# Attention scores and products with V on small TensorE tiles, with P transposed on VectorE, in a fused attention and MoE kernel

## The chip, the cores and the metric

The kernel runs on one core of a Trainium2 chip. The metric is the device time of one execution in microseconds; before the change the median of three runs is 1303.9 (1302.64 to 1307.83).

## The reference, cut to what matters

Eight batches, eight heads, 576 positions, 64 dimensions per head, all float32. The attention is causal by blocks of 64 positions, so a query block i sees the keys of blocks 0 to i.

```python
B, H, S, D = q.shape                      # 8, 8, 576, 64
scores = (1.0 / np.sqrt(D)) * np.matmul(q, k.transpose(0, 1, 3, 2))
scores = np.where(block_i >= block_j, scores, -1e9)      # blocks of 64
attn = np.exp(scores - scores.max(-1, keepdims=True))
attn = attn / (attn.sum(-1, keepdims=True) + 1e-09)
x = np.matmul(attn, v)                    # -> 4608 tokens x 512
h = np.maximum(x @ w_in, 0.0)             # 512 -> 2048
x = h * h @ w_out                         # 2048 -> 512
# then a soft mixture: 32 slots from all tokens, 8 experts on 4 slots each, slots back to tokens
```

## The kernel before, in words

The work is written as a list of operations, each with an engine, a cost in ns, what it reads and writes, and a due time; `Program.order` (L95) plays them through a model of the engines and gives one static order per engine. Among the operations that are ready, an engine takes the one with the earliest due time. The order of TensorE, VectorE, ScalarE and SP is therefore fixed before the run, and a late operand stalls whatever stands behind it on its engine.

Three kinds of work are interleaved. The MLP runs over 12 chunks of 384 tokens and, in each, over 16 slots of 128 hidden units. A slot is 12 matmuls into the bank HB (`slot_h`, L647: the weight and the activation are each split into a high and a low fp32r part, three products for each of four parts), the relu and square on ScalarE, a new split on VectorE (L656, L658), and nine matmuls of 512 columns into three banks (`slot_o`, L672). Slots are due 5 units apart (`t_at`, L793). The low parts of the weights are read again from memory for each slot (L640, `WL`, three buffers).

The attention runs as jobs of two heads, four jobs per batch (`job`, L362); from batch 2 on there are 24 whole jobs (L829 to L832), due 6 slots apart, some slots ahead of the MLP chunk that needs their tokens. A job loads q and k transposed for both heads (L381) and V (L392, L396); makes a rounded copy and a residue of q and k (L400, L403); makes the scores of query tiles of 64 and 128 rows as two fp32r products each (L437); takes negated row maxima on VectorE (L460), exponentials with row sums on ScalarE (L476), scales P by the reciprocal of the sums on either engine (L492, L493); transposes P in 25 blocks of 128x128 on TensorE (L513), copies them from PSUM (L516, L517); and multiplies with V in float32: two 64x64 products for query block 0 (L529), products with 64 output rows for one head beside the other (L539), and full-array ones for the diagonal blocks (L547). The result goes to `xr` (L554), from which `x_split` (L613) makes the chunk's operands. Four PSUM banks (pool "w") serve all jobs and the mixture, `moe2` (L698), which runs once per chunk with three-tile products (L727, L779).

After the last chunk come the experts and the output, bound by the loads of the expert weights at first (L943); `keep_warm` (L990) puts idle transposes into the gap there.

Of the kernel before, what the change touches and what calls it, by code (L numbers as in the profile page):

```python
# [38 lines left out]
class Op:  # L39
    __slots__ = ("alts", "eng", "cost", "fn", "due", "n", "nwait", "pred", "succ", "start", "end", "grp", "take",  # L40
                 "give", "nbytes", "waits", "cls")


class Program:
# [17 lines left out]

    def add(self, alts, r=(), w=(), due=0.0, grp=None, take=False, give=False, nbytes=0, after=(), waits=(), sets=None, cls=None):

        o = Op()
        o.alts = alts if isinstance(alts, list) else [alts]
        o.due, o.n, o.cls = due, len(self.ops), cls
        o.succ, o.grp, o.take, o.give, o.nbytes, o.waits = [], grp, take, give, nbytes, waits
        pred = dict.fromkeys(after, True)
        if grp is not None:  # L70
            w = tuple(w) + (grp,)
# [12 lines left out]
        for k in r:  # L84
            self.readers.setdefault(k, []).append(o.n)
        for k in w:
            self.last_w[k] = o.n
            self.readers[k] = []
        o.pred = pred
        self.ops.append(o)  # L90
        if sets is not None:
            self.events.setdefault(sets, []).append(o.n)
        return o.n

    def order(self, banks):  # L95
# [6 lines left out]
        ready = {e: [] for e in engs}  # L102
        dma_free = 0.0
        bank_at = {k: [0.0] * n for k, n in banks.items()}
        parked = {k: [] for k in banks}
        ops = self.ops

# [42 lines left out]
        while True:  # L150
            best, be = None, None
            for e in engs:
                if ready[e]:
                    t = free[e]
                elif future[e]:
                    t = max(free[e], future[e][0][0])
                else:
                    continue
                if best is None or t < best:
                    best, be = t, e  # L160
            if be is None:
                break
            t = best
            while future[be] and future[be][0][0] <= t:
                _, n = heapq.heappop(future[be])
                heapq.heappush(ready[be], (ops[n].due, n))
            _, n = heapq.heappop(ready[be])
            o = ops[n]
            if o.take:
                at = bank_at[o.grp.pool]  # L170
                i = min(range(len(at)), key=lambda j: at[j])
                if at[i] == float("inf"):
                    parked[o.grp.pool].append(n)
                    continue
                if at[i] > t:
                    heapq.heappush(future[be], (at[i], n))
                    continue
                o.grp.bank = i
                at[i] = float("inf")
            o.start = t  # L180
            load[be] -= o.cost
            if be == "sp" and o.cost:
                free[be] = t + 475.0
                dma_free = max(dma_free, t + 1160.0) + o.nbytes / 360.0
                o.end = dma_free + 900.0
            else:
                o.end = run_pe(t, o.cost) if be == "pe" else t + o.cost
# [25 lines left out]
def c_mm(n):  # L213
    return max(109.0, n / 2.4 + 13)


def c_mm4(n):

    return 4 * max(53.0, n / 2.4) + 56

# [11 lines left out]


def c_tt(n):
    return 66 + 1.04 * n


def emit(tc, qk, v, vd, w, phi, w1, w2, jsel, gsel, out):
    nc = tc.nc
# [119 lines left out]
    def parts(i):  # L359
        return range(2) if i == 4 else range(1)  # L360

    def job(L, b, p, ti, due0, due1, plain=False):  # L362
# [137 lines left out]
        for gi, g, bats, at in plan(ti):  # L500
# [23 lines left out]
            if g[0] == 0:  # L524
                c = at[(2, 0, 0)]

                def mm(gr=gr, c=c):
                    for h in range(2):
                        pe.matmul(bank(gr)[64 * h:64 * h + 64, 0:64], L.VD[0:64, 1 - h, 0:64],  # L529
                                  L.PT[0:64, c + 64 * h:c + 64 * h + 64], start=True, stop=True)  # L530
                prods.append((c_mm4(64), mm, [c // 64, c // 64 + 1], K("VD")))
            for kt in range(g[-1]):
# [8 lines left out]
                prods.append((c_mm4(w_), mm, [x for c in cs for x in range(c // 64, (c + w_) // 64)], K("V")))  # L541
            for i in g:
                if i:
                    c = at[(2, i, i)]

                    def mm(gr=gr, i=i, c=c, o=Q0[i] - q_, last=i == g[-1]):
                        pe.matmul(bank(gr)[:, o:o + 128], L.VD[:, i + 1], L.PT[:, c:c + 128], start=False, stop=last)  # L547
                    prods.append((220, mm, [c // 64, c // 64 + 1], K("VD")))
            for x, (cost, mm, pts, vk) in enumerate(prods):
                pr.add(("pe", cost, mm), r=[vk] + [K("PT", y) for y in pts], grp=gr, take=(x == 0),  # L550
                       waits=old if x == 0 else ())
            r0 = (b % 2) * S + q_
# [26 lines left out]
    def w_decode(ft, due, to, after=()):  # L579

        lt, lk = to
        for j in range(2):
            t, rk = raws(ft, j)

            def part_(x, t=t):
# [8 lines left out]

            pr.add(("act", c_act(N, True), lambda c=c, part_=part_: act.activation(c, f(part_(1)), AF.Abs)),
                   r=rk, w=[ck], due=due)
            pr.add(("act", c_act(N, True), lambda q_=q_, part_=part_: act.activation(q_, part_(0), AF.Copy, scale=2.0 ** -29)),
                   r=rk, w=[qk_], due=due)
# [99 lines left out]
    def moe2(c, m, due):  # L698
# [25 lines left out]
        for k in range(KT):  # L724
            def mm(k=k, g=g):
                for t in range(NTT):
                    pe.matmul(bank(g)[32 * t:32 * t + 32, 0:128], ph[:, k], xT[:, k, t * 128:(t + 1) * 128],  # L727
                              start=(k == 0), stop=(k == KT - 1))
            pr.add(("pe", 270, mm), r=YAK + ["ph"], grp=g, take=(k == 0), due=due)
        M, nM, sE = T("M"), T("nM"), T("sE")  # L730
# [49 lines left out]
        pr.add(("pe", 912, mm), r=[("X2", t) for t in range(NTT)] + ["ET"], grp=g, take=True, due=due)  # L780
        if m == 0:
# [15 lines left out]
    lane_init(L0)  # L797
    lane_init(L1)
    lane_b = []
    for n in range(2):  # L800
# [74 lines left out]
    one = ident[0:1, 0:1]  # L875
    lR = [("a", nm, h) for h in range(2) for nm in ("hk", "hq", "ql")]
    lF = [("a", "V"), ("a", "VD")] + [("a", "P", h, i, z_) for h in range(2) for i in range(5) for z_ in parts(i)]
# [3 lines left out]
    aR = []  # L881

    def in_R(i):
        if not aR:
            aR.append(cp.tile([128, 6 * S], F32, name="aR2", tag="aR"))
        return aR[0][:, 1024 * i:1024 * (i + 1)]

# [106 lines left out]

    keep_warm(36, HB, "HB", due + 200)
    z = (NCH - 1) % 2
# [233 lines left out]
def layout(inp):  # L1230
# [7 lines left out]
    kq = np.stack([kk.reshape(B * H, S, D), q.reshape(B * H, S, D)], axis=1).transpose(0, 3, 1, 2).reshape(B * H, D, 2 * S)  # L1238
    kq = c(np.concatenate([kq, kq], axis=1))
    vb = v_.reshape(B * H // 2, 2, 9, 64, D)  # L1240
    vf = vb[:, :, 0:8].reshape(-1, 2, 4, 2, 64, D).copy()
# [18 lines left out]
    return dict(qk=kq, v=vf, vd=vdiag, w=w, phi=ph, w1=w1, w2=w2, jsel=J.reshape(96, 64), gsel=G.reshape(128, 2, 96))  # L1260

# [15 lines left out]
```

## Time and profile before

| | us |
|---|---|
| median of 3 runs | 1303.9 |
| the profiled execution | 1306.84 |
| its span, first to last instruction | 1305.1 |
| TensorE busy (share of the span) | 1255.4 (96%) |
| VectorE busy | 764.9 (59%) |
| ScalarE busy | 714.6 (55%) |
| mean granted TensorE clock | 0.984 of 2.4 GHz |

Busy time counts matmuls from start to modelled end, and they overlap, so sums of durations are more than the time they take; the chain of work that ended last gives each line the time that it adds. Shares of busy time are means over stretches with different limits; the stretches are read one by one. Durations of VectorE and ScalarE instructions hold some latency that the next one overlaps.

### The profile page before, as it was taken

Reading aid. Unit: us, or ns where it says so; the run is one execution under the profiler, and the core shown is the slowest. Engines: PE = TensorE matmul, PEld = TensorE weight load, DVE = VectorE, ACT = ScalarE, POOL = GpSimd, SP = SyncE. Lnnn points to the kernel's source line nnn. Section 1 sums busy time; section 2 is a strip of 40 time slices with the busy share of each in tenths; the row PEclk is TensorE's granted clock in tenths of the full one; section 3 lists DMA queues with packets and bytes.
Section 4 is the critical chain, followed back from the end, with each engine's and each line's share of the span. In section 5 each row is a group of like instructions: output and inputs, shape, how many; then the busy total and the mean of one; then the engine's idle time right before and its main releaser. Section 6 shows DMA issues by size and latency. Waiting matters only on the chain.

```text
span 1305.1 us, 21721 instructions
## 1 busy us (share of the span) xinstructions
PE 1255.4 (96%) x7877; PEld 1067.6 (82%) x7877; DVE 764.9 (59%) x2429; ACT 714.6 (55%) x1811; POOL 2.7 (0%) x14
## 2 busy tenths in 40 slices
PE   6879899999999999999999999999999999999994
PEld 5657788888888898888888898888888898989843
DVE  7998899846556555555557555555557543232213
ACT  6786797745555555546555545446555544232324
POOL 0000000000000000000000000000000000000000
PEclk8988999999999999999999999999999999999998
DMA  6588668443443334343433343443443336456899
GB/s 191 196 276 275 207 215 286 155 155 117 143 136 116 118 137 131 130 147 117 144 134 118 111 143 131 131 146 120 141 134 121 109 123 226 161 193 239 291 376 339
DMA packets 97643, 224.42 MB, mean 172 GB/s; under 512 B 30337, under 2 KB 42369, under 8 KB 97537
## 3 DMA queue, kind: packets, MB, share of 16 engines
q1 hardware_dynamic: 97536, 223.05, 50.4%
q8 instruction: 62, 1.02, 0.3%
q14 instruction: 45, 0.36, 0.1%
HBM read 204.40 MB, written 18.61 MB: 171 GB/s over the span
## 4 chain that ended last, share of the span: by engine, by line
PE 79%; DVE 12%; ACT 3%; DMA 3%; issue 1%; SPq 0%; ACTq 0%; DVEq 0%
PE HB L647 26%; PE O L672 26%; PE B L437 6%; PE B L512 5%; PE B L539 5%; PE B L547 3%; DVE anm L460 2%; DMA aF<-in_qk 1%; DVE aR L403 1%; PE B L712 1%; PE B L727 1%; ACT aF L476 1%; PE B L779 1%; DVE MG L658 1%; DVE X L602 1%
## 5 line engine op out<-in xcount | busy, mean ns | idle before, releaser
L647 PE MATMUL HB<-MX,W 128*128 128x384 f32 x1536 | 436.3, 343 | 4.7 <-ACT R L653 4.6
L672 PE MATMUL O<-W,MG 128*128 128x512 f32 x1152 | 338.4, 399 | 1.5 <-DVE MG L656 1.5
L647 PEld LDWEIGHTS HB<-MX,W 128*128 128x128 f32 x1536 | 281.6, 189 | 11.7 <-ACT R L653 5.4
L647 PE MATMUL HB<-MX,WL 128*128 128x384 f32 x768 | 261.6, 341 | 0.4 <-DMA WL<-wlo_d 0.2
L476 ACT ACTIVATE aF<-B,anm 128x288 f32<-128x288 f32 (+4 forms) x338 | 166.1, 496 | 159.8 <-DVE anm L466 152.2
L672 PEld LDWEIGHTS O<-W,MG 128*128 128x128 f32 x1152 | 210.1, 189 | 36.6 <-DVE MG L656 2.1
L656 DVE CAST MG<-R 128x384 fp32r<-128x384 f32 x158 | 56.3, 356 | 276.7 <-ACT R L654 276.5
L653 ACT ACTIVATE R<-HB 128x384 f32<-128x384 f32 x192 | 93.9, 489 | 162.2 <-PE HB L647 162.0
L672 PE MATMUL O<-WL,MG 128*128 128x512 f32 x576 | 167.5, 395 | 0.0
L460 DVE TENSOR_REDUCE anm<-B 128x1 f32<-128x288 f32 (+4 forms) x338 | 150.2, 449 | 7.9 <-PE B L437 1.2
L647 PEld LDWEIGHTS HB<-MX,WL 128*128 128x128 f32 x768 | 144.7, 188 | 5.9 <-issue 2.7
L437 PE MATMUL B<-aR 128*128 128x288 f32 (+5 forms) x704 | 136.6, 308 | 9.0 <-ACT aR L400 8.7
L516 ACT COPY aF<-B 128x512 f32<-128x512 f32 (+2 forms) x201 | 103.5, 537 | 60.9 <-PE B L512 59.5
L437 PEld LDWEIGHTS B<-aR 128*128 128x128 f32 (+1 forms) x704 | 109.8, 189 | 23.5 <-ACT aR L400 9.1
L512 PE MATMUL B<-ident,aF 128*128 128x128 f32 x768 | 117.9, 278 | 11.4 <-ACT aF L476 5.1
L672 PEld LDWEIGHTS O<-WL,MG 128*128 128x128 f32 x576 | 108.0, 188 | 24.8 <-issue 1.0
L512 PEld LDWEIGHTS B<-ident,aF 128*128 128x128 f32 x768 | 93.2, 143 | 26.8 <-ACT aF L476 6.9
L658 DVE TENSOR_TENSOR MG<-R,MG 128x384 fp32r<-128x384 f32 x192 | 106.5, 555 | 10.2 <-DVE MG L656 0.9
L403 DVE TENSOR_TENSOR aR<-aF,aR 64x576 fp32r<-64x576 f32 (+6 forms) x136 | 93.2, 687 | 8.9 <-ACT aR L400 6.4
L654 ACT ACTIVATE R<-R 128x384 f32<-128x384 f32 x163 | 85.8, 526 | 3.6
L539 PE MATMUL B<-aF 128*64 128x256 f32 (+1 forms) x792 | 86.2, 349 | 0.0
L492 DVE TENSOR_SCALAR aF<-aF,ari 128x192 f32<-128x192 f32 (+4 forms) x216 | 75.3, 377 | 1.8
(233 smaller groups left out, 1171.3 us busy)
## 6 DMA issues: line engine op xcount, KB each, us to landing
WL<-wlo_d SPq DMA_DIRECT2D x187, 512.0 KB, 3.3
aF<-in_qk SPq DMA_DIRECT2D x24, 1152.0 KB, 5.2
aF<-in_v SPq DMA_DIRECT2D x32, 256.0 KB, 2.8
Wr<-in_w SPq DMA_DIRECT2D x16, 512.0 KB, 4.8
aF<-in_w SPq DMA_DIRECT2D x13, 512.0 KB, 5.9
YA<-in_w SPq DMA_DIRECT2D x11, 512.0 KB, 4.6
call<-in_w SPq DMA_DIRECT2D x11, 512.0 KB, 4.5
wlo_d<-W SPq DMA_DIRECT2D x11, 512.0 KB, 5.3
```

What stands on the lines that cost most here:

```text
L403: return ("dve", c_tt(n), lambda: dve.tensor_sub(dst, a, b_))
L437: pr.add(("pe", cost, lambda a=a, k_=k_, n=n, bc=bc, j=j, rows=rows: pe.matmul(bank(gr)[rows, bc:bc + n], a, k_, start=(j == 0), stop=bool ...
L460: pr.add(("dve", c_tt(n), lambda gr=gr, n=n, bc=bc, x=x: dve.reduce_max(L.nm[:, x:x + 1], bank(gr)[:, bc:bc + n], axis=AX.X, negate=True)) ...
L476: pr.add(("act", c_act(n, ext=2), lambda gr=gr, P_=P_, z=z, n=n, bc=bc, x=x: act.activation(P_, bank(gr)[:, bc:bc + n], AF.Exp, bias=L.nm[ ...
L512: pe.transpose(bank(gr)[:, c:c + 128], L.F[:, o:o + 128], ident)
L516: pr.add([("act", c_act(c), lambda gr=gr, c=c, d_=d_: act.copy(d_, bank(gr)[:, 0:c])), ("dve", c_tt(c), lambda gr=gr, c=c, d_=d_: dve.tens ...
L539: pe.matmul(bank(gr)[64 * h:64 * h + 64, o:o + w_], L.V[:, h, 64 * kt:64 * kt + 64], L.PT[:, cs[h]:cs[h] + w_], start=(kt == 0), stop=False)
L647: pr.add(("pe", c_mm(CH), lambda a=a, b_=b_, sl=sl, n=n: pe.matmul(HB[:, 0:CH], (WL[i] if a == "l" else W[ft])[:, sl], b_, start=(n == 0), ...
L653: pr.add(("act", c_act(CH), lambda: act.activation(r_, HB[:, 0:CH], AF.Relu)), w=["HB", ("r", j)], due=-1)
L654: pr.add([("act", c_act(CH, True), lambda: act.activation(r_, r_, AF.Square)), ("dve", c_tt(CH), lambda: dve.tensor_mul(r_, r_, r_))], w=[ ...
L658: pr.add(("dve", c_tt(CH), lambda: dve.tensor_sub(gl, r_, f(gh))), r=[("r", j), ("gh", j)], w=[("gl", j)], due=-1)
L672: pr.add(("pe", c_mm(512), lambda a=a, b_=b_, sl=sl, t=t, p_=p_: pe.matmul(OB[t], a[:, sl], (WL[i] if b_ == "l" else W[ft])[:, 512:1024], ...
```

## The change

From batch 2 on `job` is replaced by `job64`. Keys, queries and V come in two loads, in layouts in which each head or each half of the keys has its own 64 partitions. The scores are unsplit float32 products: a matmul takes 64 partitions of one head, 32 queries and every second block of 32 keys, so that a query tile of 64 rows lies in 128 partitions as two halves of the queries times two halves of the keys. The maxima and sums of the two key halves are brought together by one product with a permutation (`swap_q`) and nine small operations. P is scaled and transposed in place on VectorE, in blocks of 32x32. The products with V are float32 with 64 partitions of keys and 64 outputs each; two banks take the two query halves. The planner knows three tiled modes of the array beside the full one, a cost of changing between them (95 ns in, 195 ns back) and a preference of 2.0 due units for staying; an operation may take two banks at once; some costs are set anew; the warm-up in the tail has 30 transposes for 36. Batches 0 and 1 keep `job`.

```diff
+INTO, BACK, STAY = 95.0, 195.0, 2.0
...
+            if be == "pe":
+                _, n = heapq.heappop(min((x for x in modes if x), key=lambda x: (x[0][0] + (0 if x is modes[mode] else STAY), x[0][1])))
...
+                c = o.cost
+                if be == "pe" and o.mode != mode:
+                    mode = o.mode
+                    c += INTO if mode else BACK
+                o.end = run_pe(t, c) if be == "pe" else t + c
...
+def c_tr(n):
+    return 100 + 1.08 * n
...
+    PT9, PH_ = 256, 2336
+    PHASES = [[8, 6], [7, 5, 1], [4, 3, 2, 0]]
...
+    def job64(b, p, due0, due1):
...
+        def P_(i):
+            return L0.F[:, 0:2 * PH_].rearrange("p (h n) -> p h n", h=2)[:, :, PT9 * i:PT9 * i + 32 * i + 32]
...
+        pr.add(("sp", 50, lambda: sp.dma_start(kq(), kq2[n2])), w=[K("kq", z)], nbytes=8 * S * 128, after=oldR)
+        pr.add(("sp", 50, lambda: sp.dma_start(v_2(), v2[n2])), w=[K("v2")], nbytes=8 * S * 128, after=oldR)
+        for ph_ in PHASES:
+            gs = [Group("w") for _ in range(2)]
...
+            for i in ph_:
+                def mm(i=i, gs=gs, c=col[i]):
+                    for g in range(4):
+                        q_, a = divmod(g, 2)
+                        for h in range(2):
+                            x = kq()[64 * h:64 * h + 64]
+                            pe.matmul(bank(gs[h])[32 * g:32 * g + 32, c:c + 32 * i + 32].rearrange("p (b n) -> p b n", n=32),
+                                      x[:, S + 64 * i + 32 * q_:S + 64 * i + 32 * q_ + 32],
+                                      x[:, 0:S].rearrange("p (b a n) -> p b a n", a=2, n=32)[:, 0:i + 1, a], start=True, stop=True)
+                pr.add(("pe", max(110.0, 53.4 * (i + 1)), mm), r=[K("kq", z)], grp=gs, take=(i == ph_[0]), mode=2,
+                       after=oldF + pv_end if i == ph_[0] else ())
...
+                    pr.add(("dve", c_tt(n), lambda g=gs[h], n=n, c=c, x=x: dve.reduce_max(
+                        St[:, 0, x:x + 1], bank(g)[:, c:c + n], axis=AX.X, negate=True)), w=[K("nm2", x)], grp=gs[h])
...
+                    pr.add(("act", c_act(n, ext=2), lambda g=gs[h], n=n, c=c, x=x, i=i, h=h: act.activation(
+                        P_(i)[:, h], bank(g)[:, c:c + n], AF.Exp, bias=St[:, 0, x:x + 1], scale=0.125,
+                        accum_out=St[:, 1, x:x + 1])),
+                        r=[K("nm2", x)], w=[K("P2", i, h), K("sm2", x)], grp=gs[h], give=(i == ph_[-1]))
...
+        pr.add(("pe", 222, lambda: pe.matmul(bank(g)[:, 0:36], swap_q, Z[:, 0:36], start=True, stop=True)),
...
+        for i in range(9)[::-1]:
...
+            pr.add([("dve", c_tt(2 * n), lambda i=i, n=n, x=x: dve.tensor_mul(
+                P_(i), P_(i), fct[:, x:x + 2].unsqueeze(2).to_broadcast([128, 2, n]))),
+                ("act", 2 * c_act(n, True, 1), n_act)], r=[K("f", 4)], w=[K("P2", i, h) for h in range(2)], cls="n3")
+            pr.add(("dve", c_tr(2 * n), lambda i=i: dve.transpose(P_(i), P_(i))), w=[K("P2", i, h) for h in range(2)])
...
+        for k in range(9):
+            def mm(k=k):
+                for q_ in range(2):
+                    for h in range(2):
+                        sl, o = slice(64 * q_, 64 * q_ + 64), PH_ * h + (PT9 + 32) * k
+                        pe.matmul(bank(gs[q_])[64 * h:64 * h + 64, 32 * k:288].rearrange("p (i n) -> p i n", n=32),
+                                  v_2()[sl, h, 64 * k:64 * k + 64],
+                                  L0.F[sl, o:o + PT9 * (9 - k)].rearrange("p (i n) -> p i n", n=PT9)[:, :, 0:32],
+                                  start=(k == 0), stop=(k == 8))
+            pr.add(("pe", 2 * max(56.0, 26.7 * (9 - k)), mm), r=[K("v2")] + [K("P2", i, h) for i in range(k, 9) for h in range(2)],
+                   grp=gs, take=(k == 0), waits=old if k == 0 else (), mode=3)
+        pv_end[:] = [len(pr.ops) - 1]
...
     for b in range(2, 8):
         for p in range(4):
             d = t_at(FT * (1.5 * b - 2) + 6 * p) - 0
-            job(L0, b, p, [0, 1, 2, 3, 4], d, d + 6 * TS)
+            job64(b, p, d, d + 6 * TS)
...
-    keep_warm(36, HB, "HB", due + 200)
+    keep_warm(30, HB, "HB", due + 200)
```

The key columns that a tile a of the keys takes are blocks of 32 with a step of 64, and P of tile i starts 256 columns after that of tile i - 1, so the operands that stream are runs of 32 values.

## Rows read from the trace of the kernel before

**Rows 1.** Stretches: window, length, busy us (x instructions) per engine, clock share, DMA share, GB/s
```profile
core 0: us, PE busy (x) PEld busy (x) DVE busy (x) ACT busy (x) POOL busy (x), PEclk, DMA share, GB/s
...
600.00:700.00 100.00, 100.00 (x625) 87.05 (x624) 54.85 (x179) 51.51 (x135) 0.00 (x0) 1.00 0.40 134
1100.00:1200.00 100.00, 99.95 (x529) 88.69 (x524) 27.05 (x65) 29.28 (x62) 0.00 (x0) 1.00 0.56 197
```

**Rows 2.** The chain that ended last: shares of the span by engine and by line
```profile
PE 79%; DVE 12%; ACT 3%; DMA 3%; issue 1%; SPq 0%; ACTq 0%; DVEq 0%
PE HB L647 26%; PE O L672 26%; PE B L437 6%; PE B L512 5%; PE B L539 5%; PE B L547 3%; DVE anm L460 2%; DMA aF<-in_qk 1%; DVE aR L403 1%; PE B L712 1%; PE B L727 1%; ACT aF L476 1%; PE B L779 1%; DVE MG L658 1%; DVE X L602 1%
```

**Rows 3.** The chain in order of time, 712 to 727 us: start, us, what
```profile
712.57 2.08 PE O L672 x9
...
714.75 0.26 PE B L529 x4
715.02 0.80 PE B L539 x8
715.82 0.64 PE B L547 x4
716.46 0.44 PE B L512 x4
716.90 2.11 PE HB L647 x12
...
722.38 1.66 PE B L539 x16
724.04 0.64 PE B L547 x4
```

**Rows 4.** Two neighbouring jobs in the timeline, and L647's matmuls between them
```profile
749.81 0.27 PE L529 MATMUL B<-aF 64*64 64x64 f32 x2
...
784.91 0.27 PE L529 MATMUL B<-aF 64*64 64x64 f32 x2
...
749.81:784.91 35.10, 13.77 (x72) 12.45 (x72) 1.00 0.40 136
```

**Rows 5.** Products on column tiles in the timeline: start, us, engine, line, shapes, count
```profile
708.19 0.15 PEld L779 LDWEIGHTS B<-X,ET 128*32 128x32 f32 x6 [0.16 <-issue]
...
1242.12 0.63 PE L1049 MATMUL O<-aR,YA 128*32 128x512 f32 x3
1242.14 0.62 PE L1049 MATMUL O<-aF,YA 128*32 128x512 f32 x1
1242.58 0.60 PE L1049 MATMUL O<-aR,YA 128*32 128x512 f32 x3
...
1239.40 0.64 PE L1032 MATMUL B<-s,J 96*32 96x1 f32 x16
```

**Rows 6.** Groups of VectorE and ScalarE instructions by shape: xcount | busy us, mean ns
```profile
L516 ACT COPY aF<-B 128x512 f32<-128x512 f32 x165 | 93.8, 591 | 50.2 <-PE B L512 48.9
L476 ACT ACTIVATE aF<-B,anm 128x288 f32<-128x288 f32 x128 | 63.1, 499 | 6.9 <-DVE anm L469 6.9
L460 DVE TENSOR_REDUCE anm<-B 128x1 f32<-128x288 f32 x128 | 56.8, 450 | 2.3 <-PE B L437 0.6
L476 ACT ACTIVATE aF<-B,anm 128x448 f32<-128x448 f32 x60 | 37.9, 632 | 23.2 <-DVE anm L466 23.2
L460 DVE TENSOR_REDUCE anm<-B 128x1 f32<-128x448 f32 x60 | 37.1, 618 | 1.1
L655 DVE TENSOR_TENSOR R<-R 128x384 f32<-128x384 f32 x29 | 15.8, 545 | 0.5 <-ACT R L653 0.5
L484 DVE TENSOR_SCALAR ari<-asm 128x1 f32<-128x1 f32 x64 | 13.2, 206 | 2.0 <-ACT aF L476 1.9
L618 DVE CAST MX<-xr 128x384 fp32r<-128x384 f32 x35 | 11.8, 353 | 9.0 <-PE HB L647 8.5 <-ACT xr L554 0.4
```

**Rows 7.** DMA issues on SP: what, xcount, KB each, median us from issue to landing
```profile
WL<-wlo_d SPq DMA_DIRECT2D x187, 512.0 KB, 3.3
aF<-in_qk SPq DMA_DIRECT2D x24, 1152.0 KB, 5.2
```

More of the change, by code (lines that the diff above doesn't have):

```diff
@@ L40 @@
     __slots__ = ("alts", "eng", "cost", "fn", "due", "n", "nwait", "pred", "succ", "start", "end", "grp", "take",
-                 "give", "nbytes", "waits", "cls")
+                 "give", "nbytes", "waits", "cls", "mode")
 class Program:
@@ L61, in __init__, with add @@
         self.events = {}
-    def add(self, alts, r=(), w=(), due=0.0, grp=None, take=False, give=False, nbytes=0, after=(), waits=(), sets=None, cls=None):
+    def add(self, alts, r=(), w=(), due=0.0, grp=None, take=False, give=False, nbytes=0, after=(), waits=(), sets=None, cls=None, mode=0):
         o = Op()
         o.alts = alts if isinstance(alts, list) else [alts]
-        o.due, o.n, o.cls = due, len(self.ops), cls
+        o.due, o.n, o.cls, o.mode = due, len(self.ops), cls, mode
         o.succ, o.grp, o.take, o.give, o.nbytes, o.waits = [], grp, take, give, nbytes, waits
@@ L105, in order @@
         parked = {k: [] for k in banks}
+        keep = {}
         ops = self.ops
@@ L152, in order @@
             for e in engs:
-                if ready[e]:
+                if ready[e] or (e == "pe" and any(modes)):
                     t = free[e]
@@ L165, in order @@
                 _, n = heapq.heappop(future[be])
-                heapq.heappush(ready[be], (ops[n].due, n))
-            _, n = heapq.heappop(ready[be])
+                heapq.heappush(modes[ops[n].mode] if be == "pe" else ready[be], (ops[n].due, n))
+            if be == "pe":
+                _, n = heapq.heappop(min((x for x in modes if x), key=lambda x: (x[0][0] + (0 if x is modes[mode] else STAY), x[0][1])))
+            else:
+                _, n = heapq.heappop(ready[be])
             o = ops[n]
             if o.take:
[L170 to L173, printed above, removed]
+                gs = o.grp if isinstance(o.grp, list) else [o.grp]
+                pool = gs[0].pool
+                at = bank_at[pool]
+                js = sorted(range(len(at)), key=lambda j: at[j])[:len(gs)]
+                kept = keep.get(pool)
+                if at[js[-1]] == float("inf") or kept not in (None, n) and ops[kept].due < o.due:
+                    parked[pool].append(n)
+                    if len(gs) > 1 and kept is None:
+                        keep[pool] = n
                     continue
-                if at[i] > t:
-                    heapq.heappush(future[be], (at[i], n))
+                if at[js[-1]] > t:
+                    heapq.heappush(future[be], (at[js[-1]], n))
                     continue
-                o.grp.bank = i
-                at[i] = float("inf")
+                if kept == n:
+                    keep[pool] = None
+                for g_, i in zip(gs, js):
+                    g_.bank = i
+                    at[i] = float("inf")
             o.start = t
@@ L213, in c_mm @@
 def c_mm(n):
-    return max(109.0, n / 2.4 + 13)
+    return max(109.0, n / 2.26 + 4.5)
 def c_mm4(n):
-    return 4 * max(53.0, n / 2.4) + 56
+    return 2 * max(103.0, n / 1.2)
 def c_act(n, sbuf=False, ext=0):
@@ L540, in mm @@
                                   L.PT[:, cs[h]:cs[h] + w_], start=(kt == 0), stop=False)
-                prods.append((c_mm4(w_), mm, [x for c in cs for x in range(c // 64, (c + w_) // 64)], K("V")))
+                prods.append((c_mm4(w_), mm, [x for c in cs for x in range(c // 64, (c + w_) // 64)], K("V"), 1))
             for i in g:
@@ L547, in mm @@
                         pe.matmul(bank(gr)[:, o:o + 128], L.VD[:, i + 1], L.PT[:, c:c + 128], start=False, stop=last)
-                    prods.append((220, mm, [c // 64, c // 64 + 1], K("VD")))
-            for x, (cost, mm, pts, vk) in enumerate(prods):
+                    prods.append((222, mm, [c // 64, c // 64 + 1], K("VD"), 0))
+            for x, (cost, mm, pts, vk, md) in enumerate(prods):
                 pr.add(("pe", cost, mm), r=[vk] + [K("PT", y) for y in pts], grp=gr, take=(x == 0),
-                       waits=old if x == 0 else ())
+                       waits=old if x == 0 else (), mode=md)
             r0 = (b % 2) * S + q_
@@ L728, in mm @@
                               start=(k == 0), stop=(k == KT - 1))
-            pr.add(("pe", 270, mm), r=YAK + ["ph"], grp=g, take=(k == 0), due=due)
+            pr.add(("pe", 206, mm), r=YAK + ["ph"], grp=g, take=(k == 0), due=due, mode=1)
         M, nM, sE = T("M"), T("nM"), T("sE")
@@ L779, in mm @@
                 pe.matmul(bank(gs)[32 * t:32 * t + 32], ET[:, 32 * t:32 * t + 32], X2[t], start=True, stop=True)
-        pr.add(("pe", 912, mm), r=[("X2", t) for t in range(NTT)] + ["ET"], grp=g, take=True, due=due)
+        pr.add(("pe", 856, mm), r=[("X2", t) for t in range(NTT)] + ["ET"], grp=g, take=True, due=due, mode=1)
         if m == 0:
@@ L880, in emit @@
     pr.add(("sp", 50, lambda: sp.dma_start(J, jsel)), w=["J"], due=TE, nbytes=1 << 15)
-    aR = []
     def in_R(i):
-        if not aR:
-            aR.append(cp.tile([128, 6 * S], F32, name="aR2", tag="aR"))
-        return aR[0][:, 1024 * i:1024 * (i + 1)]
+        return a_r()[:, 1024 * i:1024 * (i + 1)]
     room = [(lambda i=i: in_R(i), lR, ()) for i in range(6 * S // 1024)]
```

101 lines of the change are left out of this document (92 added, 9 removed).

## The prediction

> **What bounds the kernel now.** I read the stretches first. In a stretch amid the attention jobs TensorE is busy 100% of the time at a granted share of 1.00 (the 2.4 GHz level), while VectorE stands at 55% and ScalarE at 52%; after the last attention job they fall to 27% and 29% and TensorE stays at 100% [rows 1]. So in those stretches each microsecond less of TensorE is a microsecond less of span, if nothing else takes its place. The shares of the chain say the same: 79% of the span is TensorE, and the lines of the attention job (L437, L512, L539, L547) hold 19 points of it, the MLP lines L647 and L672 52 [rows 2].
>
> What one attention job costs TensorE I take from the chain in order of time. Its products with V come in two pieces, 0.26 + 0.80 + 0.64 and 1.66 + 0.64 us, together 4.00 [rows 3]. Four transposes take 0.44, so one takes 0.109, and a job has 25: 2.73 [rows 3]. The whole job is checked by the pitch: the same matmul of two neighbouring jobs starts at 749.81 and 784.91, which is 35.10 us, and in between lie 72 matmuls of L647, six MLP slots [rows 4]. A slot is 2.11 for L647 and 2.08 for L672 [rows 3], so six are 25.1 and the job is **10.0 us**. The scores are what is left, 3.3 us for 24 products.
>
> **The change, part by part.** Only the 24 jobs from batch 2 on change; the opening, the MLP and the tail keep their work.
>
> *Transposes leave TensorE*: 2.73 us a job less there.
>
> *Scores on 64x32 tiles.* Each of nine query tiles issues eight float32 matmuls, one per array tile, of 32(i+1) columns. A float32 matmul shows as two instructions, two passes: the three products of L779 are six weight loads [rows 5]. A pass of 128 columns takes 0.109, as do the transposes above [rows 3], so 32 columns take 0.0272. If all eight tiles run side by side, the scores take 2 x 45 x 0.0272 = 2.45 us. Four column tiles do run side by side: their four matmuls start within 0.02 us, and the next pass comes 0.46 us later, for 512 columns [rows 5]; 0.02 over three steps is 7 ns per tile. Eight tiles at 7 ns are 0.056 per pass, which binds only the two smallest query tiles: 2.5 us in all. That two halves of the rows also run side by side no row shows. From below, nothing is cheaper than this streaming; from above, the halves go one after the other, 5.0. I take 2.5: loads and matmuls of four tiles overlap freely, and this is the nearest row.
>
> *Products with V on 64x64 tiles.* Nine steps of four tiles of 32(9-k) columns: again 2 x 45 x 0.0272, with the smallest step held to a weight load, 2.5 us, and 5.0 from above for the same reason.
>
> *The swap of the statistics* is one full-array float32 product, half of L547's 0.44 pair [rows 3]: 0.22.
>
> *Changing the array's shape.* In the second piece of V products the eight passes (six of 256 columns, two of 128) should stream 6 x 0.218 + 2 x 0.109 = 1.53 and take 1.66: 0.13 to enter. The four 128-column passes after them should take 0.44 and take 0.64: 0.20 to return [rows 3]. A visit is 0.33. Three score phases and one run of V products make four visits, 1.3 us. The planner could do with two (0.7) or need eight (2.6), because only a preference of 2.0 in due time holds a run together.
>
> *Sum on TensorE*: 2.5 + 2.5 + 0.22 + 1.3 = 6.6 us against 10.0, so 3.4 us a job and 24 x 3.4 = **82 us**.
>
> *Work moved to VectorE and ScalarE.* VectorE loses the split of queries and keys (L400 and L403), ScalarE most of the copies out of PSUM (L516, 0.59 each) [rows 6]. Before, a period holds 0.5485 x 35.1 = 19.3 us of VectorE, of which the MLP alone makes 0.27 x 25.1 = 6.8 [rows 1], so a job uses 12.5. After it: 18 maxima, by L460's two sizes 0.148 us and 1.05 us per thousand columns, over 2880 columns: 5.7; some ten small operations at L484's 0.2: 2.0; the scaling by L655's size 4.3, half of it on ScalarE: 2.1; a copy, 0.5 [rows 6]. The 32x32 transposes have no row. Below, a cast of 384 columns takes 0.353, or 2.7 us for 2880; above, two sweeps at the price of L655, 8.6; I take one sweep, 4.3, since like L655 they read and write float32 in SBUF [rows 6]. Together 14.6, and with the MLP 21.4 of a new period of 31.7: 68%. ScalarE's 18 exponentials cost 0.26 us and 0.83 us per thousand columns by L476 [rows 6], 7.1, with half of the scaling about 10.7, and 18 of 31.7 with the MLP. Both lie beside TensorE, which always has an MLP slot to run; I cost them at nothing. The Trainium skill (Vector Engine (DVE) Microarchitecture Reference, section 3.8) says that the 32x32 transpose sustains one element per cycle and lane; with 0.96 GHz (Trainium Kernel Development and Optimization, NeuronCore Architecture) 2880 columns would be an estimated 3.0 us plus starts, no run here shows it, and the sum would be the same.
>
> *If that cover goes*, the job's own chain shows. P has one buffer: the first scores of a job wait for the last V product of the one before, and the first V product reads all nine tiles, so nothing of two jobs overlaps but loads. The chain: scores and first maxima 2.5, exponentials 7.1, statistics 2.5, half of the scaling and the transposes 6.4, V products 2.8. With ScalarE and VectorE lent to the MLP for 27 to 29% [rows 1] the middle ones stretch to 10 and 9: 27 us of 31.7. That leaves almost 5 us.
>
> *Loads.* A job loaded 1152 + 256 KB and the diagonal blocks in four transfers; now two of 576 KB each. V has one buffer, so its transfer waits on SP for the last V product, with the weight loads of L640 queued behind it. Those land in 3.3 us, the query and key load in 5.2 [rows 7], and three weight buffers stand ahead of need, two slots or 8 us, so a wait of some us is hidden. Fewer warm-up transposes in the tail (30 for 36) and corrected planner costs I cost at nothing: MLP slots fill the planner's gaps, and without that cover six transposes are 0.65 us, 6 x 0.109.
>
> The profiled execution took 1306.84 us (span 1305.1), 2.9 over the median 1303.9. 1306.84 - 82 = 1225, against the median **1222 us**.
>
> **The rivals.**
>
> 1. *The two row halves take turns.* Place: every pass of scores and V products. Price: 5.0 us more a job, 11.6 against 10.0, and 24 x 1.6 = 38 us slower: 1342. It decides once the tiled passes take more than (10.0 - 1.5) / 5.0 = 1.7 times the streaming time. For it: no product before uses both halves with K = 64 (L529's two tiles both read the lower half). Against: the four column tiles do not take turns [rows 5].
>
> 2. *Issue binds the small tiles.* Sixteen instructions per query tile may not go out at 7 ns. The farthest row is L1032, sixteen one-column matmuls in 0.64 us, about 0.47 from first to last start (0.64 less a last one of 0.17), 31 ns each [rows 5]. Then a score step costs at least 0.50, nine of them 4.5, and a V step at least 0.25, 2.9 in all: 2.4 us more a job, 1222 + 58 = 1280. Against it, the 7 ns of the same engine with columns to stream. The Trainium skill (TensorE: Matmul & The Clock Gate, Part 1) puts a floor of about 25 ns from start to start however few the columns; by that rule the estimate would be 1.4 us more a job, 1257. The four starts within 0.02 us do not agree with it for different tiles.
>
> 3. *The chain of the job becomes the period.* If the transposes take two sweeps, the chain grows by 4.3 / 0.73 = 6 us to 33, over the 31.7; with the latencies between engines that I left out, some 33.5, and 24 x 1.8 = 43 us come back: 1265. For it: one buffer of P. Against: the MLP may run some slots ahead of a late job.
>
> 4. *The tiles run but the planner scatters them*, or TensorE waits at the head of its queue for a late exponential: eight visits give 24 x 1.3 = 32 us back, 1254. The change then does not do what it says, few long runs.
>
> **How the numbers follow.** The forecast, with its own spread of 1203 (two visits) to 1245 (six visits, some waits), has 0.68; rival 1 0.09, rival 2 0.08, rival 3 0.08, rival 4 0.07. The range 1200 to 1275 leaves out rival 1, the far half of rival 2 and the ends of the forecast's own spread that I may have drawn too narrow, under 2 in 10 together. A measurement of this kernel can tell about 0.5%, 6.5 us, from no change. All cases but rival 1 are faster by more than that; rivals 2 and 3 at worse prices together can eat the gain, so I put faster at 0.87, within 0.5% at 0.03 and slower at 0.10.
>
> **What would show it.** In the changed trace the eight matmuls of a score pass should start within some 0.06 us and the nine steps of scores fill about 2.5 us on the chain, V products 2.5; if they take 5 each, rival 1 is right, and if only the small tiles are slow, rival 2. The pitch of jobs with six slots between should be near 31.7. TensorE should stay at 99 to 100% in the stretches between 300 us and the end of the jobs, at a granted share of 1.00: idle time ended by the exponential or the transpose speaks for rival 3. The transposes should sum to about 4.3 us a job on VectorE, which should read 65 to 70% busy. Four visits a job should show as four groups of tiled matmuls. The prediction is wrong if TensorE stays full and the time is not below 1275: then a tiled pass costs more than its columns.

## The result, and the profile after the change

The changed kernel takes 1217.03 us (four runs, 1216.77 to 1221.3); the ratio to the kernel before is 0.934 (95% interval 0.931 to 0.937). The profiled execution took 1216.88 us with a span of 1215.1, 90 us less than before.

First the stretches of the changed kernel, one amid the jobs and one after them (columns as in [rows 1]):

```profile
600.00:700.00 100.00, 99.78 (x1087) 85.52 (x1089) 59.55 (x187) 50.93 (x183) 0.00 (x0) 1.00 0.42 134
1000.00:1100.00 100.00, 99.36 (x541) 86.22 (x541) 29.63 (x74) 32.04 (x70) 0.00 (x0) 1.00 0.60 213
```

TensorE is as full as before and its granted share still 1.00; VectorE rose from 55 to 60%, ScalarE stayed at 51%. So TensorE is still the bound, and less work stands on it. The chain in order of time shows one period of a job (L447 is now the scores, L470 the swap, L501 the products with V; L808 and L833 are the MLP's L647 and L672):

```profile
674.05 1.89 PE B L447 x80
675.94 2.30 PE HB L808 x12
678.24 2.08 PE O L833 x9
680.32 2.10 PE HB L808 x12
682.42 0.98 PE B L447 x52
683.41 2.30 PE O L833 x9
...
689.90 0.14 PE B L470 x2
...
699.91 2.64 PE B L501 x72
...
705.53 1.89 PE B L447 x80
```

From one job's first scores to the next's is 705.53 - 674.05 = 31.48 us, against 35.10 in [rows 4], again with 72 matmuls of the first MLP line between them:

```profile
674.05:705.53 31.48, 14.07 (x72) 12.58 (x72) 1.00 0.43 137
```

That is 3.62 us a job, and 24 x 3.62 = 87 us, which is also the difference of the two medians (1303.9 - 1217.0). In the two traces the difference is 90, and it arises in the stretch of the jobs: the last MLP slot that starts ahead of the first job's scores starts at 204.0, and the same slot at 204.1 in the kernel before. Which jobs hold the 3 us beyond 24 equal periods is not worked out. At the end of the MLP the 90 are complete; its last matmuls start at 1142.8, and started at 1232.6 in the kernel before, 89.8 later. The tail behind it is as long as it was (1215.1 - 1142.8 = 72.3 and 1305.1 - 1232.6 = 72.5). The line's summary after the change:

```profile
L833 PE MATMUL O<-W,MG x1152: 387/393/505, 56.5 to 1142.8; 128*128 128x512 f32 x192
```

and before it:

```profile
L672 PE MATMUL O<-W,MG x1152: 387/393/511, 61.0 to 1232.6; 128*128 128x512 f32 x192
```

How the eight tiles run is seen in a narrow piece of the timeline, up to 705.53, with the mean of one such matmul from the groups by shape below it:

```profile
705.46 0.47 PE L447 MATMUL B<-aR 64*32 64x288 f32 x8
...
L447 PE MATMUL B<-aR 64*32 64x288 f32 x384 | 17.2, 415 | 0.0
```

Eight matmuls of about 0.42 us fit into 0.47: they start within some 0.05 us, about 7 ns apart, two halves of the rows and four column tiles at once. The maxima (L456) and the transposes that are now on VectorE, these all together and at two sizes:

```profile
L456 DVE TENSOR_REDUCE aF<-B 128x1 f32<-128x192 f32 (+8 forms) x432 | 111.0, 316 | 79.4 <-PE B L447 79.1
...
L493 DVE STREAM_TRANSPOSE aF<-aF 128x256 f32<-128x256 f32 (+8 forms) x216 | 95.9, 486 | 0.5
...
L493 DVE STREAM_TRANSPOSE aF<-aF 128x576 f32<-128x576 f32 x24 | 18.5, 771 | 0.0
L493 DVE STREAM_TRANSPOSE aF<-aF 128x128 f32<-128x128 f32 x24 | 7.3, 303 | 0.0
```

The slope of the transposes is (771 - 303) / 448 = 1.04 ns per column, one sweep.

### The profile page after: what moved, and what is told of

Read it like the earlier page. It is cut to its first block, busy times and chain, and to the rows that moved or that the text cites. A ratio compares the mean times of both kernels' runs of the same rounds, so it can differ in the third digit from the quotient of the medians.

```text
span 1215.1 us, 28105 instructions
## 1 busy us (share of the span) xinstructions
PE 1165.3 (96%) x11063; PEld 973.4 (80%) x11063; DVE 730.8 (60%) x2282; ACT 657.1 (54%) x2079; POOL 3.0 (0%) x16
## 4 chain that ended last, share of the span: by engine, by line
PE 84%; DVE 8%; DMA 3%; ACT 2%; issue 1%; SPq 0%; ACTq 0%; DVEq 0%
PE HB L808 32%; PE O L833 31%; PE B L447 6%; PE B L501 5%; DVE anm L621 1%; DMA aF<-in_qk 1%; PE B L873 1%; PE B L888 1%; PE B L940 1%; PE O L1210 1%; PE B L598 1%; DVE aR L564 1%; DMA WL<-wlo_d 1%; DVE X L763 1%; PE B L1265 1%
## 5 line engine op out<-in xcount | busy, mean ns | idle before, releaser
L808 PE MATMUL HB<-MX,W 128*128 128x384 f32 x1536 | 441.4, 345 | 2.6 <-ACT R L814 1.7
L833 PE MATMUL O<-W,MG 128*128 128x512 f32 x1152 | 339.2, 398 | 1.1 <-DVE MG L817 1.0
L808 PEld LDWEIGHTS HB<-MX,W 128*128 128x128 f32 x1536 | 281.4, 189 | 18.0 <-issue 4.0
L808 PE MATMUL HB<-MX,WL 128*128 128x384 f32 x768 | 261.4, 340 | 0.8 <-DMA WL<-wlo_d 0.6
L833 PEld LDWEIGHTS O<-W,MG 128*128 128x128 f32 x1152 | 211.2, 188 | 38.8 <-issue 3.6
L463 ACT ACTIVATE aF<-B,aF 128x192 f32<-128x192 f32 (+8 forms) x432 | 166.9, 414 | 115.2 <-DVE aF L458 112.7
L833 PE MATMUL O<-WL,MG 128*128 128x512 f32 x576 | 167.4, 395 | 0.0
L456 DVE TENSOR_REDUCE aF<-B 128x1 f32<-128x192 f32 (+8 forms) x432 | 111.0, 316 | 79.4 <-PE B L447 79.1
L808 PEld LDWEIGHTS HB<-MX,WL 128*128 128x128 f32 x768 | 144.9, 189 | 10.0 <-DMA WL<-wlo_d 2.6
L833 PEld LDWEIGHTS O<-WL,MG 128*128 128x128 f32 x576 | 107.8, 188 | 25.7 <-issue 1.3
L463 ACT ACTIVATION_READ_ACCUMULATOR aF<-B,aF 128x1 f32 x432 | 97.2, 225 | 0.0
L493 DVE STREAM_TRANSPOSE aF<-aF 128x256 f32<-128x256 f32 (+8 forms) x216 | 95.9, 486 | 0.5
L447 PEld LDWEIGHTS B<-aR 64*32 64x32 f32 x3456 | 57.6, 105 | 22.2 <-issue 13.6
L447 PE MATMUL B<-aR 64*32 64x192 f32 (+8 forms) x3456 | 73.7, 301 | 0.0
L514 ACT COPY xr<-B 128x288 f32<-128x288 f32 x48 | 16.8, 403 | 100.0 <-PE B L501 100.0
L489 ACT ACTIVATE aF<-aF 128x256 f32<-128x256 f32 (+4 forms) x146 | 56.1, 435 | 26.1 <-DVE aF L483 26.1
L501 PEld LDWEIGHTS B<-aF,aR 64*64 64x64 f32 x1728 | 52.3, 133 | 18.7 <-issue 10.0
L501 PE MATMUL B<-aF,aR 64*64 64x192 f32 (+8 forms) x1728 | 66.4, 301 | 0.0
```

Of the source, the lines that this page charges most:

```text
L447: pe.matmul(bank(gs[h])[32 * g:32 * g + 32, c:c + 32 * i + 32].rearrange("p (b n) -> p b n", n=32), x[:, S + 64 * i + 32 * q_:S + 64 * i + ...
L456: pr.add(("dve", c_tt(n), lambda g=gs[h], n=n, c=c, x=x: dve.reduce_max(St[:, 0, x:x + 1], bank(g)[:, c:c + n], axis=AX.X, negate=True)), ...
L463: pr.add(("act", c_act(n, ext=2), lambda g=gs[h], n=n, c=c, x=x, i=i, h=h: act.activation(P_(i)[:, h], bank(g)[:, c:c + n], AF.Exp, bias=S ...
L489: act.activation(P_(i)[:, h], P_(i)[:, h], AF.Copy, scale=fct[:, x + h:x + h + 1])
L493: pr.add(("dve", c_tr(2 * n), lambda i=i: dve.transpose(P_(i), P_(i))), w=[K("P2", i, h) for h in range(2)])
L501: pe.matmul(bank(gs[q_])[64 * h:64 * h + 64, 32 * k:288].rearrange("p (i n) -> p i n", n=32), v_2()[sl, h, 64 * k:64 * k + 64], L0.F[sl, o ...
```

## The experiments

Twelve kernels ran, each an edit of the changed one; the diffs are cut to the lines that matter. Times are medians, to be set against 1217.0; ratios are to the kernel before the change, 1303.9 to 1306.3 in the same sessions.

**1. Scores with the row halves in turn.**

```diff
-            for i in ph_:
-                def mm(...):              # for g in range(4): for h in range(2): matmul(i, g, h)
+            for h in range(2):
+                def mm(...):              # for i in ph_: for g in range(4): matmul(i, g, h)
```

> The changed kernel with one edit: in each score phase all query tiles of the first head (lower half of the rows) are issued ahead of all those of the second head (upper half), so the two row halves take turns; nothing is left out. Theory (the eight tiles run side by side and TensorE is the bound): the streaming of the scores, 2.6 us a job, is paid twice less a small overlap where the halves meet, 2.3 to 2.6 us more a job, 24 jobs, so 1217 + 55 to 62 = 1272 to 1279 us. Rival (the halves take turns already, and the gain came from the transposes that left TensorE, 24 x 2.73 = 66 us, and from the fewer columns): no change, 1217.

Measured 1247.2 (ratio 0.956, 0.954 to 0.958): 30 us slower, half of what the theory asked and far from the rival's zero. With this edit the planner sees each half of a phase as one operation, where each query tile was one, so its order can differ as well. The chain shows the first two phases at 2.35 where they took 1.89, and the pitch of two jobs at 32.73, which is 1.25 more, or 24 x 1.25 = 30 us:

```profile
691.44 2.35 PE B L448 x76
...
724.17 2.35 PE B L448 x76
```

The third phase grew by about 0.4 likewise (1.39 for 0.98); the last 0.4 of the 1.25 is not assigned. Full turns of the first two phases would be about 3.6, twice 1.74 of streaming (columns times 0.0272) and the 0.13 of entry. Two narrow pieces of the timeline of the same place say why; the windows end at 724.14 and 724.20:

```profile
724.10 0.45 PE L448 MATMUL B<-aR 64*32 64x288 f32 x4
...
724.10 0.50 PE L448 MATMUL B<-aR 64*32 64x288 f32 x8
```

The four tiles of the first half start, and 0.05 us later those of the second half have started too, although the first half has 16 matmul passes ahead of them in the program (288 and 224 columns, two passes each, four tiles), of which 12 had not started. So program order alone did not make the halves take turns; a half can be issued past what still waits in the other. The run is a weaker test than it was meant to be, and it rules out the rival all the same.

**2. The products with V in turn as well.**

```diff
-        for k in range(9):
-            def mm(k=k):                  # for q_ in range(2): for h in range(2): matmul(k, q_, h)
+        for q_ in range(2):
+            def mm(q_=q_):                # for k in range(9): for h in range(2): matmul(k, q_, h)
```

> As the run before, and the products with V likewise: all steps of the first half of the rows, then all of the second; nothing is left out. This is rival 1 of the prediction made on purpose. Theory: some 2.3 to 2.5 us a job more than the run before, so 1217 + 110 to 122 = 1327 to 1339 us, slower than the kernel before the change (1304). Rival (halves take turns already): 1217.

Measured 1302.5 (0.999, 0.998 to 1.000), as long as the kernel before and not slower than it; the expected 1327 was missed by the same 25 us by which run 1 missed its 1272. The step from run 1 is 1302.5 - 1247.2 = 55 us, 2.3 a job, as the theory had it, and on the chain a run of V products takes 4.96 where it took 2.64, 2.32 more. The order moved too (in most jobs the first two score phases fall apart), so the agreement of 55 with 24 x 2.32 = 56 holds smaller terms that cancel. The timeline up to 716.83 and up to 716.86 shows the point at which the second half begins:

```profile
714.57 4.96 PE B L502 x70
...
714.50 2.54 PE L502 MATMUL B<-aF,aR 64*64 64x288 f32 x29
...
714.50 2.80 PE L502 MATMUL B<-aF,aR 64*64 64x288 f32 x32
```

The end of the group jumps by 0.26 because a long matmul of the second half, 288 columns, has started; 30 of the first half's 36 had, three passes per tile still to go. In the score phases of the first run the second half also began when three passes per tile were left (at once in the phase that has only four). With long runs the halves do take turns, and their running side by side is worth 2.3 of the 2.5 us of streaming.

**3. No transposes.**

```diff
-            pr.add(("dve", c_tr(2 * n), lambda i=i: dve.transpose(P_(i), P_(i))), w=[K("P2", i, h) for h in range(2)])
```

> The changed kernel without the 32x32 transposes on VectorE: P goes into the products with V untransposed, so this part of the computation is left out. Theory (VectorE's work lies beside TensorE's): 1217 within 5 us, although 4.0 us a job of VectorE are gone. Rival (the chain of the job over scores, exponentials, scaling, transposes and products with V sets the period): up to 24 x 4.0 = 96 us faster, and anything under 1200 speaks for it.

Measured 1219.2 (0.934, 0.933 to 0.936): the same. VectorE fell from 60 to 50% amid the jobs, and the time did not move:

```profile
600.00:700.00 100.00, 100.00 (x1116) 85.46 (x1112) 50.40 (x161) 48.99 (x179) 0.00 (x0) 1.00 0.41 136
```

The transposes are hidden, and the chain of the job does not set the period.

**4 and 5. More transposes.** The first has the transposes of the even query tiles three times, the second all of them.

```diff
-            pr.add(("dve", c_tr(2 * n), lambda i=i: dve.transpose(P_(i), P_(i))), ...)
+            for _ in range(3 if i % 2 == 0 else 1):        # second: range(3)
+                pr.add(("dve", c_tr(2 * n), lambda i=i: dve.transpose(P_(i), P_(i))), ...)
```

> The changed kernel with each transpose of query tiles 0, 2, 4, 6 and 8 done three times, which gives the same P; the planner is told of it. VectorE gets 10 more transposes a job over 3200 columns, about 4.4 us. Theory (the chain of the job has almost 5 us to spare of its period): 1217 to 1235 us. Rival (VectorE's time is on the path): 24 x 4.4 = 106 us more, 1323.

> The changed kernel with every transpose done three times, same P, the planner told: 18 more a job over 5760 columns, about 8.0 us of VectorE. Theory (one buffer of P makes the chain of a job, about 27 us of the 31.5 us period, the limit once some 5 us are added): the chain grows by 8.0 / 0.73 = 11 us to 38, 6.5 over the period, 24 x 6.5 = 156 less what the MLP can run ahead (some 40): about 1290 to 1370 us. Rival (only the sum of VectorE's work counts, and (60% of 31.5 + 8.0) / 31.5 = 85% still fits): 1217 to 1225.

Measured 1232.4 (0.945, 0.944 to 0.947) and 1299.8 (0.997, 0.996 to 0.998), both inside the theory's bounds and far from the rivals' 1323 and 1225. Two stretches of the second, one of its waits, and the line of TensorE that waits longest:

```profile
500.00:600.00 100.00, 93.57 (x1017) 79.85 (x1017) 67.84 (x206) 48.99 (x174) 0.00 (x0) 0.94 0.37 121
700.00:800.00 100.00, 83.24 (x967) 68.34 (x953) 72.95 (x218) 46.65 (x169) 0.00 (x0) 0.93 0.34 112
...
778.30:792.70 14.40, 0.09 (x7) 0.07 (x5) 14.08 (x38) 2.01 (x6) 0.00 (x0) 0.62 0.00 1
...
L502 PE MATMUL B<-aF,aR 64*64 64x192 f32 (+8 forms) x1728 | 73.2, 323 | 44.0 <-issue 44.0
```

VectorE is at 68 to 73%, far from full, and yet TensorE stands idle 44 us ahead of the products with V, in three waits of up to 15 us. In such a wait VectorE is busy 14.08 of 14.40 us, nearly all of it with scaling and transposing P, and TensorE has no MLP slot left ahead of these products in its order. So the chain through the one buffer of P binds there, and not the sum of VectorE's work. The granted share of TensorE's clock is 0.62 over that wait and 0.50 in its last 4 us (the 1.2 GHz level), and the V products behind it take 4.02 us on the chain for 2.64. The 44 us are half of the 83 that this run lost; the rest is not split up. The first of the two has no such idle time; its stretch of jobs grew by 10.6 us (from 760.5, by the first and last swap). It has 24 more runs of tiled matmuls, but only 7 more returns to the full array, since the others begin right behind the products with V; at 0.37 us (run 6) these 7 are 2.6 us. What lengthened the rest of its time is not settled.

**6. No preference for staying in a mode.**

```diff
-INTO, BACK, STAY = 95.0, 195.0, 2.0
+INTO, BACK, STAY = 95.0, 195.0, 0.0
```

> The changed kernel with the planner's preference for staying in a mode set from 2.0 to 0 due units; the work is the same, its order is not. Theory: runs of tiled products break up, from 3.5 visits a job to about 6, and each costs 0.33 us, so 24 x 2.5 x 0.33 = 20 us more, 1237 us; whatever the number of visits turns out to be, the time should move by 0.33 us per visit added. Rival (changing the array's shape costs nothing beside what overlaps it): 1217.

Measured 1250.0 (0.958, 0.957 to 0.960). The phases fall apart in the chain, five visits for the scores where there were two:

```profile
656.30 1.02 PE B L447 x32
...
659.62 0.92 PE B L447 x32
...
662.84 0.27 PE B L447 x16
...
665.40 0.43 PE B L447 x16
...
668.12 0.71 PE B L447 x40
```

Counting runs of L447 and L501 in the traces (a run ends where any other matmul, or the other of the two lines, starts), the changed kernel has 84 (3.5 a job), this one 148. The first and last start of the swap bound the stretch of the jobs; here the changed kernel's line and then this run's:

```profile
L470 PE MATMUL B<-aF x48: 193/248/279, 224.5 to 985.0; 128*128 128x36 f32 x48
```

```profile
L470 PE MATMUL B<-aF x48: 193/248/279, 232.7 to 1016.7; 128*128 128x36 f32 x48
```

The stretch grew from 760.5 to 784.0, 23.5 us for 64 visits, 0.37 each; the estimate was 0.33. The whole time moved by 33 where 20 were expected. The other 8 us lie ahead of the first job, where the new setting also orders the work of batches 0 and 1 anew and the granted share between 100 and 200 us is 0.91 instead of 0.95.

**7, 8 and 9. More preference for staying**: 8.0, 5.0, and 8.0 only from 215 us of planned time on.

```diff
-INTO, BACK, STAY = 95.0, 195.0, 2.0
+INTO, BACK, STAY = 95.0, 195.0, 8.0     # next: 5.0; then 8.0 where t > 215e3, 2.0 before
```

> The changed kernel with the planner's preference for staying in a mode set from 2.0 to 8.0 due units. Theory: the first two score phases of a job follow the V products of the one before without a return to the full array, so 3.5 visits a job become about 2.5 and 24 x 1.0 x 0.3 = 7 us go: 1210 us. Rival (the longer runs of attention work make the MLP's chain or the banks of the mixture late, and TensorE waits): 1217 or slower.

> As the run before with the preference at 5.0 due units, between the two. Theory: between 1210 and 1217 us, by 0.3 us per visit saved. Rival: 1217 or slower.

> The changed kernel with the planner's preference for staying in a mode at 8.0 due units from 215 us of planned time on and at 2.0 before, since with 8.0 throughout the stretch of the attention jobs got 3.9 us shorter and the opening 10.4 us longer. Theory (returns to the full array cost what the chain shows): 1217 - 4 = 1213 us. Rival (the longer opening was the price of the same order and comes back elsewhere): 1217 or slower.

Measured 1222.3 (0.938, 0.936 to 0.939), 1217.3 (0.934, 0.932 to 0.935) and 1219.4 (0.933, 0.931 to 0.936). The lines of the swap for 8.0 throughout and for 8.0 from 215 us on:

```profile
L470 PE MATMUL B<-aF x48: 193/274/300, 234.9 to 991.4; 128*128 128x36 f32 x48
```

```profile
L470 PE MATMUL B<-aF x48: 193/274/300, 229.1 to 993.2; 128*128 128x36 f32 x48
```

With 8.0 the stretch is 756.5, 4.0 shorter, but begins 10.4 later. With 8.0 from 215 us on it is 764.1, longer than before, and still begins 4.6 late; the profiled execution was the slowest of five, 4.8 over their median, so part of this may be that execution's own. My expectation of 1213 failed, and so did 1210 for 8.0: an order of the whole list is not made of independent pieces, and why the stretch lost what it had won is open. The planner did save returns to the full array (80 in the changed kernel; 69, 59 and 67 in these three), yet with 59 of them the time is 1217.3. So 0.37 us a visit is what added visits cost in run 6; that saving one gives it back is not shown. No setting beats 2.0.

**10. TensorE's transposes put back, idle.** 25 transposes of the identity per job, the rest as changed.

```diff
+        gd = Group("w")
+        for y in range(5):
+            def idle_tr(gd=gd):
+                for _ in range(5):
+                    pe.transpose(bank(gd)[:, 0:128], ident, ident)
+            pr.add(("pe", 5 * 109, idle_tr), r=["id"], grp=gd, take=(y == 0), give=(y == 4))
```

> The changed kernel with 25 full-array transposes of the identity into a spare PSUM bank added to each of the 24 jobs, in five operations that the planner knows of: TensorE gets back the 2.73 us a job that the transposes of P took, and nothing else. Theory (TensorE's time is the span's in the stretch of the jobs): 1217 + 24 x 2.73 = 1282 us, a little more for the bank that they hold. Rival (TensorE is no longer the bound after the change, the chain of the job is): less than half of it, under 1250.

Measured 1259.8 (0.966, 0.964 to 0.968): 43 us more, neither 65 nor under 33. The added line by stretches:

```profile
0.00:130.00 130.00, 28.00 (x200) 25.22 (x200) 0.97 0.73 238
...
230.00:1030.00 800.00, 49.30 (x400) 45.59 (x400) 1.00 0.39 125
```

Since the transposes read nothing but the identity, a third of them was planned into the opening, where TensorE had idle time (busy 99.5 of the first 130 us without them, 118.7 with them); the first swap starts at 224.2 as against 224.5. The 400 that lie among the jobs are 400 x 0.109 = 43.6 us, and the time grew by 43. Microsecond for microsecond, TensorE's work in that stretch is the span.

**11 and 12. The small edits.** The first has the old costs of the planner and 36 warm-up transposes, the second only these.

```diff
-    return max(109.0, n / 2.26 + 4.5)      # c_mm; likewise c_mm4 and five single costs
+    return max(109.0, n / 2.4 + 13)
...
-    keep_warm(30, HB, "HB", due + 200)
+    keep_warm(36, HB, "HB", due + 200)
```

> The changed kernel with the planner's old costs for matmuls, weight decoding and the mixture, and 36 warm-up transposes in the tail for 30; the work of the jobs and the modes stay as changed. Theory (these edits are worth nothing): 1217 within 6 us. Rival (part of the gain came from a better plan): more than 6 us slower.

> The changed kernel with 36 warm-up transposes in the tail for 30, all else as changed. With the old costs as well, the tail became 8.8 us longer, because warm-up transposes kept the bank HB and the last products of the first expert layer were ordered behind those of the second. Theory A (the six more transposes alone do that): 1217 + 9 = 1226 us. Theory B (they cost their own 0.65 us, and the order comes from the costs): 1217 to 1218 us.

Measured 1226.3 (0.940, 0.937 to 0.942) and 1225.4 (0.938, 0.936 to 0.941). So the six transposes alone cost about 8 us, and the old costs nothing that can be told. Of the 8, 7 lie in the tail, which is 79.5 us long for 72.3 (1223.8 - 1144.3, from the last start of an MLP matmul to the end). The end of the chain of the last run (L1154 is the warm-up, L1210 the first expert layer, L1253 the second):

```profile
1167.75 5.31 PE B L1253 x80
1173.06 1.73 PE B L1265 x32
...
1175.82 0.33 PE HB L1154 x3
1176.15 3.61 PE HB L1210 x32
```

and of the changed kernel, in which the last warm-up transpose starts at 1150.1:

```profile
1152.09 7.89 PE O L1210 x72
...
1161.01 0.99 PE HB L1210 x8
...
1169.04 6.17 PE B L1253 x88
```

The warm-up transposes write the bank HB and have the latest due time. Those that the gap does not hold are ordered late, and the last 32 products of the first expert layer, which need that bank, wait behind them: they start at 1176.15 instead of from 1161.01 on, behind most of the second layer.

## Why the prediction was right, and where its terms were off

The forecast of 1222 missed by 5 us, inside its own spread, and its mechanism held: TensorE is the bound, a microsecond of its work is one of span (run 10), and the transposes moved to VectorE are hidden (run 3). That the miss is so small is in part luck, since errors offset each other, as the terms show.

- *The job before*, 10.0 us, rests on 25.1 of MLP in a period, and the changed kernel supports that: 31.48 - 25.1 leaves 6.4 for the job, and the pieces on its chain come to as much (1.89 + 0.98 + 0.14 + 2.64, and 0.7 by which the MLP pieces behind them are longer). The forecast was 6.6; its terms, 2.5 + 2.5 + 0.22 + 1.3, add up to 6.52, which would have made it 1220. Its lower end, 1203 for two visits, would by the same prices be about 1207.
- *Scores and V products*, 2.5 each: 1.89 + 0.98 less two entries of 0.13 is 2.61, and 2.64 less one is 2.51. The step taken without a row, that the two halves of the rows run side by side, is the one on which the result hung; it was a choice of the nearest row and not knowledge. Run 2 prices it: 2.3 us a job for the V products alone. Rival 1 is out.
- *The floor of small tiles*: eight starts within about 0.05 us, and so for every query tile but two. In query tiles 2 and 0, which come last in the third phase, the starts are some 16 ns apart (medians over the 24 jobs) where the others have 7, and the phase took 0.98 on the chain against 0.90 by columns, floor and entry. So rival 2's mechanism may be there, at 0.1 us a job; at 2.4 it is out. What sets the 16 ns no run shows. The row that gave 31 ns was misread: of L1032's sixteen matmuls two start by 1239.45, and after a gap of 0.31 us the other fourteen start within 0.11 us, some 8 ns apart. The Trainium skill (TensorE: Matmul & The Clock Gate, Part 1) has a floor of about 25 ns from start to start. The trace does not agree with it for matmuls on different tiles.
- *Visits*: four were forecast at 0.33, 1.3 us. A job in the steady stretch has three, since the first two score phases run together on the four banks: about 1.0. This is the term that was off, by 0.3; the swap was not (0.22 forecast, 0.14 on the chain and 0.09 on the next slot). Less the 0.1 that the scores took more, and with the sum's rounding from 6.52 to 6.6, this is the 5 us. A return costs 0.20 (L808 at 2.30 after a visit, 2.10 without), an added visit 0.37 by run 6.
- *VectorE and ScalarE*: 68 and 57% were forecast, 60 and 51% came. The groups' means hold time that the next instruction overlaps, so sums over many small instructions came out high, as in the maxima (L456 above): 432 x 316 ns would be 136.5 us, and the group fills 111.0. The price of the transposes, one sweep, 4.3 forecast, is 95.9 us for all 24 jobs, 4.0 each. The Trainium skill (Vector Engine (DVE) Microarchitecture Reference, section 3.8) gives one element per cycle and lane; at the 0.96 GHz of the Trainium skill (Trainium Kernel Development and Optimization, NeuronCore Architecture) that is an estimated 1.04 ns. The slope in the trace agrees.
- *The slack of the job's chain*, "almost 5 us": 4.4 more of VectorE a job gave no idle TensorE, though the run was 15 us longer; 8.0 more gave 44 us of it in the whole run (runs 4 and 5). Rival 3 is out for the changed kernel and stands close by.
- *Fewer warm-up transposes*, costed at nothing with 0.65 us as the price without cover. Against the kernel before, the tail did not change (72.5 and 72.3), so the forecast lost nothing by this term. What the edit is worth in the changed kernel was wrong by an order: with 36 of them it takes 1225, 8 us more, because of the order behind them (run 12). The cover named was MLP slots, but the MLP's matmuls have all started by 1142.8 and the warm-up starts after that; that the bank HB hangs on them was overlooked.

## What to carry to other kernels

Where one engine is full through a long stretch, price a change by that engine's time on the chain, per period, and check the sum against the pitch of two periods; then look for the buffer that makes the relieved work serial, because here it, and not the busy share, said how much the other engines could take. Small float32 products can be worth packing on the array in both directions: side by side, the halves of the rows were worth nearly the whole streaming time of the V products. In a planned order, run 12 suggests that filler work belongs in a bank that nothing late needs; no run tried another bank.

## What the runs showed that was not expected

Matmuls for one half of the rows start while up to three passes per tile of earlier matmuls still wait for the other half: in the first run the second half began 0.05 us behind the first, with 12 passes ahead of it not yet started, and in the second run only when three passes per tile were left. In these runs program order therefore made the halves take turns only where the runs were longer than that. And a third of the work added in run 10 vanished into the opening: filler that depends on nothing goes where the planner has room, and it measures less than it holds.
